# Routing counts over four token tiles per matmul, list products over two, and a new order at the start of the expert stage

## The chip, the cores and the metric

The kernel runs on one core of one Trainium2 chip. TensorE (PE) multiplies matrices, VectorE (DVE) and ScalarE (ACT) work element by element, GpSimd (POOL) does element work and issues the indirect DMAs, and SyncE (SP) issues the other DMAs. Each engine takes its own instructions in order and waits for the others by semaphores. The metric is the device time of one execution in microseconds; a span is the part of it that the profile shows.

## The reference

A linear attention (3072 tokens in all, 8 heads of 48) feeds an MLP (384 to 2048 to 384, leaky ReLU), and that feeds a mixture of 8 experts (384 to 1024 to 384, ReLU). The experts have a capacity of 384 tokens each, and the assignment is greedy over all pairs of token and expert:

```python
logits = x @ w_gate
order = np.argsort(-logits.flatten())
for idx in order:
    tok, e = int(idx) // E, int(idx) % E
    if assigned[tok] >= 0 or counts[e] >= cap:
        continue
    assigned[tok] = e
    counts[e] += 1
for e in range(E):
    mask = assigned == e
    out[mask] = np.maximum(x[mask] @ w1[e], 0.0) @ w2[e]
```

## The kernel before

The attention and the MLP come first; the MLP works on groups of 512 and at last 256 tokens. Every float32 product is split into high and low parts, so three matmuls stand for one.

**Routing.** Since every expert has room for just 384 tokens, the assignment is worked out as eight rounds, `route(p)` for p from 0 to 7. A round finds the expert that fills up first, its threshold, its members, and the list of their rows. Tokens lie on 128 partitions in 24 tiles. `close(p)` (line 811) narrows the threshold in 4 steps of 32 levels. A step compares each token's key with the levels (`G`, L826), counts for each expert how many tokens reach each level by 24 matmuls, one for each token tile, with the one-hot of the token's best expert as weights (`cnt`, L831), and turns the counts into the number of levels at which an expert is still full (`fl`, `Je`, `jt`, `Jm`, L836 to L840). The one-hot stands four times over, in four blocks of 32 columns, so that each block of 32 partitions gets the same counts. Then the keys are shifted (L842). After the last step the expert's number `ei`, the membership `memb` (L859) and its prefix sums `px` follow. `lists` and `compact` turn members into slots (`xi`), two one-hots `oa` and `A`, 24 matmuls (`ip`, L920), four small ones (`iw`, L926), and the row indices `idx` (L935). `next_picks` takes the members out and makes the next one-hot `oh`, which `spread` writes (L765, L766).

**Slots.** All this is written as a generator: each `yield` ends a slot, and whoever calls `next` puts a slot at that place in the engines' order. `first_route` runs route 0 against the rest of the MLP's second layer: after slot n it issues `REST[n]` steps of three matmuls (L636). Route 0 also starts the loads of the first expert's w1 on SP as soon as `ei` is known, and splits the first pieces.

**The start of the experts.** `experts` first issues the three gathers of rows (`xg`, L1111, one for each 128 tokens, on POOL), and then follows `START`, letter by letter: c is a slot of the next routes, w splits a weight piece into high and low (ScalarE copy L1104, POOL subtraction L1105), d issues the four w2 loads (L1097), t transposes a tile of x on TensorE (L1125) and copies it on ScalarE (L1127), and l forms its low part on VectorE (L1131).

**The expert loop.** For each expert p and each of its 8 blocks f of hidden units (j = 8p + f): a slot, layer 1 (L1141, 9 matmuls of 384 columns), another slot, layer 2 of two blocks earlier (L1158, 9 matmuls), then `hl` on VectorE (L1149). So route p + 1 runs in the slots beside expert p. When its indices are known, the next gathers are issued; x is transposed in the last two blocks before the expert starts. `put` (L1161) evacuates a finished expert's three output tiles and scatters them by indirect DMA (L1167).

## Time and profile before

| | us |
|---|---|
| median of 3 runs | 808.16 (806.79 to 810.96) |
| the profiled execution | 805.67 |
| its span | 803.9 |
| TensorE busy | 771.4 |
| VectorE busy | 569.8 |
| ScalarE busy | 405.6 |
| POOL busy | 282.0 |

The MLP's last group ends at about 538 us of the span, route 0 runs from about 521 to 544, and the experts' layers from 552 to the end. [...] In a timeline each row is a start, a duration, an engine, a line, the operation, what it writes and reads, and in brackets the idle time of the engine just before with what ended it.

### The profile page before, as it was taken

How to read it: one execution, taken by the hardware profiler on the slowest of the kernel's cores; microseconds unless marked ns; L12 is line 12 of the kernel's file. 1: busy time of each engine (PE TensorE's matmuls, PEld its weight loads, DVE VectorE, ACT ScalarE, POOL GpSimd, SP SyncE). 2: the span in 40 equal slices, each digit the busy share in tenths (PEclk: the TensorE clock that was granted, in tenths of full speed). 3: DMA queues.
4: the chain of work that ended last, by engine and by line, in shares of the span. 5: the costliest groups of instructions: out<-in, count | busy, mean ns of one | idle time of the engine just before them, and what ended most of it. 6: DMA issues, size and time to landing. Idle time of an engine off the chain costs nothing.

```text
span 803.9 us, 16531 instructions
## 1 busy us (share of the span) xinstructions
PE 771.4 (96%) x6139; PEld 709.6 (88%) x6139; DVE 569.8 (71%) x1536; ACT 405.6 (50%) x875; POOL 282.0 (35%) x275
## 2 busy tenths in 40 slices
PE   7999999999999999999999999986999999999996
PEld 6788887988999899988998999876899889899996
DVE  6999997897999989889884345656666666663221
ACT  4889895665444444444534455614344344344431
POOL 7888852322000000000000000016567675578661
PEclk9999999999999999999999999997999999999999
DMA  8798864512000200300200010034462462444400
GB/s 250 200 278 247 235 195 142 194 40 80 1 1 1 79 1 11 109 20 21 71 28 1 0 60 21 1 120 138 138 201 86 148 199 78 157 158 135 142 31 32
DMA packets 64584, 81.38 MB, mean 101 GB/s; under 512 B 8048, under 2 KB 55408, under 8 KB 64368
## 3 DMA queue, kind: packets, MB, share of 16 engines
q1 hardware_dynamic: 61008, 70.81, 28.3%
q0 software_dynamic: 3072, 9.44, 3.4%
q8 instruction: 50, 0.82, 0.4%
q14 instruction: 38, 0.31, 0.1%
q10 hardware_dynamic: 416, 0.00, 0.0%
HBM read 66.07 MB, written 14.16 MB: 100 GB/s over the span
## 4 chain that ended last, share of the span: by engine, by line
PE 72%; DVE 6%; issue 3%; POOL 1%; ACT 1%; another core or an unknown queue 0%; POOLq 0%; ACTq 0%; DVEq 0%
PE m L636 25%; PE ph L689 23%; PE eph L1141 10%; PE o L1158 9%; PE cnt L831 2%; PE ept L1125 1%; DVE gh L704 1%; DVE G L826 1%; POOL out_dram L1167 1%; POOL wbl L1105 1%; ACT nt L693 1%; DVE hl L1149 1%; PE ip L920 0%; ACT gh L694 0%; DVE oa L914 0%
## 5 line engine op out<-in xcount | busy, mean ns | idle before, releaser
L689 PE MATMUL ph<-xh,wah 128*128 128x512 f32 (+1 forms) x336 | 122.2, 364 | 0.8 <-ACTq L242 0.7
L689 PE MATMUL ph<-xl,wah 128*128 128x512 f32 (+1 forms) x336 | 121.9, 363 | 0.0
L689 PE MATMUL ph<-xh,wal 128*128 128x512 f32 (+1 forms) x336 | 121.8, 363 | 0.0
L693 ACT ACTIVATE nt<-ph 128x512 f32<-128x512 f32 (+1 forms) x112 | 60.1, 536 | 120.1 <-PE ph L689 109.6
L636 PE MATMUL m<-wbh,gl 128*128 128x384 f32 (+1 forms) x352 | 119.1, 338 | 0.5 <-DVE gl L715 0.5
L636 PE MATMUL m<-wbh,gh 128*128 128x384 f32 (+1 forms) x352 | 119.3, 339 | 0.0
L636 PE MATMUL m<-wbl,gh 128*128 128x384 f32 (+1 forms) x352 | 119.2, 339 | 0.0
L781 POOL COPY L<-M 128x176 f32<-128x176 f32 (+1 forms) x2 | 0.7, 357 | 329.4 <-DVE M L642 308.4
L704 DVE SCALAR_TENSOR_TENSOR gt<-nt,al,gt 128x512 f32<-128x512 f32 (+1 forms) x96 | 67.8, 706 | 50.6 <-ACT gt L694 50.6
L712 ACT CAST gh<-gt 128x512 fp32r<-128x512 f32 (+1 forms) x96 | 56.4, 587 | 72.1 <-DVE gt L704 71.2
L1144 ACT ACTIVATE hh<-eph 128x384 fp32r<-128x384 f32 x64 | 31.4, 491 | 118.5 <-PE eph L1141 108.7
L1149 DVE SCALAR_TENSOR_TENSOR hl<-eph,hh 128x384 fp32r<-128x384 f32 x64 | 35.6, 556 | 73.2 <-ACT hh L1144 72.1
L560 DVE SCALAR_TENSOR_TENSOR junk<-wt,wgb 128x384 f32<-128x384 f32 x128 | 71.3, 557 | 3.9
L689 PEld LDWEIGHTS ph<-xh,wal 128*128 128x128 f32 x336 | 63.1, 188 | 11.0
L1105 POOL TENSOR_TENSOR wal<-raw,wah 128x768 fp32r<-128x768 f32 x32 | 58.3, 1847 | 37.3 <-ACT wah L1104 35.1
L689 PEld LDWEIGHTS ph<-xh,wah 128*128 128x128 f32 x336 | 63.1, 188 | 9.1 <-ACTq L242 1.0
L715 DVE TENSOR_TENSOR gl<-gt,gh 128x512 fp32r<-128x512 f32 (+1 forms) x96 | 61.7, 643 | 12.7 <-ACT gh L712 12.6
L689 PEld LDWEIGHTS ph<-xl,wah 128*128 128x128 f32 x336 | 63.2, 188 | 7.6
L1105 POOL TENSOR_TENSOR wbl<-raw,wbh 128x768 fp32r<-128x768 f32 x32 | 58.5, 1847 | 32.0 <-ACT wbh L1104 22.4
L636 PEld LDWEIGHTS m<-wbh,gh 128*128 128x128 f32 x352 | 66.0, 188 | 3.5
L636 PEld LDWEIGHTS m<-wbl,gh 128*128 128x128 f32 x352 | 66.1, 188 | 3.3
L636 PEld LDWEIGHTS m<-wbh,gl 128*128 128x128 f32 x352 | 66.1, 188 | 0.9 <-DVE gl L715 0.9
(252 smaller groups left out, 1778.5 us busy)
## 6 DMA issues: line engine op xcount, KB each, us to landing
raw<-in_moe_w_dram SPq DMA_DIRECT2D x64, 384.0 KB
raw<-in_moe_w_in_dram SPq DMA_DIRECT2D x16, 384.0 KB
raw<-in_moe_w_out_dram SPq DMA_DIRECT2D x16, 384.0 KB
raw_r<-in_rt_dram SPq DMA_DIRECT2D x24, 224.0 KB
raw_k<-in_kc_dram SPq DMA_DIRECT2D x24, 192.0 KB
raw_v<-in_vc_dram SPq DMA_DIRECT2D x24, 192.0 KB
xd<-ysb SPq DMA_DIRECT2D x48, 96.0 KB
md<-raw SPq DMA_DIRECT2D x22, 192.0 KB
```

The costliest lines, as they stand in the source:

```text
L560: v.scalar_tensor_tensor(junk, t, 1.0, self.wgb[:, e], op0=ALU.mult, op1=ALU.mult, accum_out=wc[:, f, e:e + 1])
L636: nc.tensor.matmul(acc[t][:, :N], a[:, o], self.wb[b][:, f, :N], start=(f == 0 and n == 0), stop=(f == NF - 1 and n == 2))
L689: nc.tensor.matmul(ph[:, :T], self.wa[a][:, k, fs], b[:, k, :T], start=(n == 0), stop=(n == 8))
L693: nc.scalar.activation(nt[:, :T], ph[:, :T], AF.Relu, scale=-1.0)
L704: v.scalar_tensor_tensor(gt[:, :T], nt[:, :T], self.al[:, f:f + 1], gt[:, :T], op0=ALU.mult, op1=ALU.add)
L712: nc.scalar.copy(h, g)
L715: v.tensor_sub(l, g, h.bitcast(F32))
L1105: self.nc.gpsimd.tensor_sub(to[1], d, to[0].bitcast(F32))
L1141: self.nc.tensor.matmul(ph, w1[a][:, k, f * P:(f + 1) * P], x[b][:, k], start=(n == 0), stop=(n == 8))
L1144: self.nc.scalar.activation(hh, ph, AF.Relu)
L1149: self.nc.vector.scalar_tensor_tensor(hl, ph, 0.0, hh.bitcast(F32), op0=ALU.max, op1=ALU.subtract)
L1158: self.nc.tensor.matmul(self.acc[q], h[a][:, o], w2[b][:, f], start=(f == 0 and n == 0), stop=(f == NS - 1 and n == 2))
```

## The change

The count matmul takes four token tiles at a time: the weights hold 4 copies of a block of 4 tiles by 8 experts, the moving side 4 tiles by 32 levels, so 6 matmuls of 128 columns make a product, of whose 4 by 4 blocks the diagonal ones are wanted. VectorE transposes the 128 by 128 product in blocks of 32 by 32, which brings levels onto partitions, sums the diagonal over the four tiles (`tot`), takes the maximum over experts (`top`), transposes it, and counts the levels that are still full (`fl`, `Jm`). In the last step the flags are formed for each expert and turned back (`F`, `Je`, `jt`). All levels are compared, 32 instead of 31, with a level that no key reaches.

The list product takes two tiles at a time: 12 matmuls of 48 columns; two small copies take the diagonal, and `two`, two identities on top of each other, adds them in `iw`.

Of the slots, `lists` joins two into one; the part of `next_picks` that forms the next one-hot becomes `next_ones` and comes behind the indices, and from p = 2 on `next_picks` has a slot of its own. The expert loop takes a slot less at its first block, and asks for new indices in both slots of a block. At the start, `REST`, `PRE` and `START` are new, and the four w2 loads come first in `START`, each behind a small POOL memset of its buffer, which stands in POOL's queue behind the gathers. `put` copies all three tiles on ScalarE. The one-hots are no longer zeroed beforehand.

```diff
@@ -36,14 +36,14 @@
...
 NS = F2 // P
-REST = (1, 2, 1, 2, 1, 3, 1, 3, 2, 4, 4, 4) + (0,) * 4
+REST = (1, 2, 3, 2, 3, 2, 3, 3, 4, 0, 0, 5) + (0,) * 4
 TAIL = 1
-START = "cwwccccdtltltlc"
+START = "dcccwtwltclwtlc"
 HOLD = 2
...
 WARM = (8, 8, 4, 4)
-PRE = 2
+PRE = 1
 BASE = 6
@@ -131,19 +131,21 @@
...
         v.tensor_scalar(self.io1, io[:, :TH], 1.0, None, op0=ALU.add)
+        g.memset(self.io1[:, TH - 1:], BIG)
         self.pcol = cp.tile([P, 1], F32, name="pcol")
...
         for i in range(2):
-            t = self.rp.tile([P, NTT, 4, 32], BF, name=f"ohr{i}")
-            for a in range(0, NTT, 6):
-                g.memset(t[:, a:a + 6].rearrange("p a b e -> p (a b e)").bitcast(F32), 0.0)
-            self.ohr.append(t)
+            self.ohr.append(self.rp.tile([P, NTT // 4, 4, 4 * E], BF, name=f"ohr{i}"))
+        self.F = cp.tile([P, 32], F32, name="F")
+        g.memset(self.F, 0.0)
+        self.two = cp.tile([2 * TH, TH], F32, name="two")
+        v.tensor_tensor(self.two, self.ident[:2 * TH, :TH], self.ident[:2 * TH, TH:2 * TH], op=ALU.add)
         S = self.S = self.ps.tile([P, 512], F32, name="S")
...
         self.xi, self.bi5, self.ai5 = (S[:, 96 + 24 * i:120 + 24 * i].bitcast(I32) for i in range(3))
-        self.iot = S[:, 168:192]
+        self.iot, self.jt = S[:, 168:192], S[:, 192:224]
         v.memset(S[:, 56:58], 0.0)
@@ -759,31 +761,44 @@
...
         t = self.ohr[i % 2]
-        if act is None:
-            nc.vector.tensor_copy(t[:, :, 0, :E], eq)
-        else:
-            nc.vector.tensor_tensor(t[:, :, 0, :E], eq, self.bc3(act, E), op=ALU.mult)
-        nc.scalar.copy(t[:, :, 1:, :E], t[:, :, 0:1, :E].to_broadcast([P, NTT, 3, E]))
+        nc.vector.tensor_tensor(self.first(t), self.fours(eq),
+                                act.rearrange("p (k g) -> p k g", g=4).unsqueeze(3).to_broadcast([P, NTT // 4, 4, E]),
+                                op=ALU.mult)
+        nc.scalar.copy(t[:, :, 1:], t[:, :, 0:1].to_broadcast([P, NTT // 4, 3, 4 * E]))
         return t
 
+    def first(self, t):
+        return t[:, :, 0].rearrange("p k (g e) -> p k g e", g=4)
+
+    def fours(self, a):
+        return a.rearrange("p (k g) e -> p k g e", g=4)
+
     def picks(self, a, b):
...
         v = self.nc.vector
-        key, eq, oh, w = self.kap[:, a:b], self.eq[:, a:b], self.oh[:, a:b], b - a
+        key, eq, w = self.kap[:, a:b], self.eq[:, a:b], b - a
         M = self.M[:, a:b]
...
         yield
-        v.tensor_copy(oh[:, :, 0, :E], eq)
-        self.nc.scalar.copy(oh[:, :, 1:, :E], oh[:, :, 0:1, :E].to_broadcast([P, w, 3, E]))
+        for c, d in ((a, b - b % 4), (b - b % 4, b)) if a % 4 == 0 else ((a, b),):
+            if a % 4 == 0 and d % 4 == 0:
+                o, e4, sh = self.oh[:, c // 4:d // 4], self.eq[:, c:d].rearrange("p (k g) e -> p k (g e)", g=4), \
+                    [P, (d - c) // 4, 3, 4 * E]
+                v.tensor_copy(o[:, :, 0], e4)
+                self.nc.scalar.copy(o[:, :, 1:], o[:, :, 0:1].to_broadcast(sh))
+            elif d > c:
+                o = self.oh[:, c // 4, :, E * (c % 4):E * (c % 4) + E * (d - c)]
+                v.tensor_copy(o[:, 0], self.eq[:, c:d].rearrange("p t e -> p (t e)"))
+                self.nc.scalar.copy(o[:, 1:], o[:, 0:1].to_broadcast([P, 3, E * (d - c)]))
         self.nc.gpsimd.tensor_copy(self.L[:, a:b], M)
...
             n = min(6, b - i)
-            v.tensor_tensor(self.G0[:, i:i + n, :TH - 1], self.bc3(self.kap[:, i:i + n], TH - 1),
-                            self.bc1(self.T[:, 0, :TH - 1], n), op=ALU.is_ge)
+            v.tensor_tensor(self.G0[:, i:i + n], self.bc3(self.kap[:, i:i + n], TH), self.bc1(self.T[:, 0], n),
+                            op=ALU.is_ge)
             yield
@@ -815,32 +830,41 @@
...
         for s in range(STEPS):
-            n = TH if s == last else TH - 1
             if p == s == 0:
...
                 G = rp.tile([P, NTT, TH], BF, name="G")
-                cuts = (0, NTT // 2) if p == 0 else (0,)
-                for t in cuts:
-                    w = NTT // len(cuts)
-                    v.tensor_tensor(G[:, t:t + w, :n], self.bc3(kap[:, t:t + w], n), self.bc1(self.T[:, s, :n], w),
+                w = NTT // 2 if p == 0 else NTT
+                for t in range(0, NTT, w):
+                    v.tensor_tensor(G[:, t:t + w], self.bc3(kap[:, t:t + w], TH), self.bc1(self.T[:, s], w),
                                     op=ALU.is_ge)
             yield
-            cnt = self.pc.tile([P, TH], F32, tag="cnt", name="cnt")
-            for t in range(NTT):
-                nc.tensor.matmul(cnt[:, :n], oh[:, t].rearrange("p b e -> p (b e)"), G[:, t, :n],
-                                 start=(t == 0), stop=(t == NTT - 1))
+            cnt = self.pc.tile([P, 4, TH], F32, tag="cnt", name="cnt")
+            for k in range(NTT // 4):
+                nc.tensor.matmul(cnt, oh[:, k].rearrange("p r x -> p (r x)"), G[:, 4 * k:4 * k + 4],
+                                 start=(k == 0), stop=(k == NTT // 4 - 1))
             yield
-            fl = rp.tile([P, TH], BF, name="fl")
-            Je = rp.tile([P, 1], F32, name="Je")
-            v.tensor_scalar(fl[:, :n], cnt[:, :n], float(CAP), None, op0=ALU.is_ge, op1=ALU.add, accum_out=Je)
-            jt = rp.tile([P, 32], F32, name="jt")
-            v.transpose(jt, Je.to_broadcast([P, 32]))
+            tr = rp.tile([P, 4 * (TH + E)], F32, name="tr")
+            v.transpose(tr[:, :P], cnt.rearrange("p g n -> p (g n)"))
+            tot = rp.tile([P, E], F32, name="tot")
+            v.tensor_reduce(tot, tr.rearrange("p (g x) -> p x g", g=4)[:, :E], axis=AX, op=ALU.add)
             Jm = rp.tile([P, 1], F32, name="Jm", bufs=2)
-            v.tensor_reduce(Jm, jt[:, :E], axis=AX, op=ALU.max)
             if s < last:
+                top = rp.tile([P, 1], F32, name="Je")
+                v.tensor_reduce(top, tot, axis=AX, op=ALU.max)
+                v.transpose(self.jt, top.to_broadcast([P, 32]))
+                fl = rp.tile([P, TH], F32, name="fl")
+                v.scalar_tensor_tensor(fl, self.jt, float(CAP), self.ones48[:, :TH], op0=ALU.is_ge, op1=ALU.mult,
+                                       accum_out=Jm)
                 v.scalar_tensor_tensor(kap, Jm.to_broadcast([P, NTT]), self.nd[:, s:s + 1], kap, op0=ALU.mult,
                                        op1=ALU.add)
+        v.tensor_scalar(self.F[:, :E], tot, float(CAP), None, op0=ALU.is_ge)
+        v.transpose(self.jt, self.F)
+        Je = rp.tile([P, 1], F32, name="Je")
+        v.tensor_reduce(Je, self.jt, axis=AX, op=ALU.add)
+        jt = rp.tile([P, 32], F32, name="jt")
+        v.transpose(jt, Je.to_broadcast([P, 32]))
+        v.tensor_reduce(Jm, jt[:, :E], axis=AX, op=ALU.max)
         v.tensor_scalar(sel, jt[:, :E], Jm, None, op0=ALU.is_equal)
@@ -852,7 +876,8 @@
...
         po3 = rp.tile([P, NTT, E], F32, name="eq")
-        v.tensor_tensor(po3, oh[:, :, 0, :E], self.bc1(sel), op=ALU.mult)
+        v.tensor_tensor(self.fours(po3), self.first(oh),
+                        sel.unsqueeze(1).unsqueeze(1).to_broadcast([P, NTT // 4, 4, E]), op=ALU.mult)
         po = rp.tile([P, NTT], F32, name="ch")
@@ -863,11 +888,16 @@
...
 
-        v, rp = self.nc.vector, self.rp
+        v = self.nc.vector
         v.tensor_tensor(self.act, self.act, self.memb, op=ALU.subtract)
...
             v.tensor_reduce(self.kap, self.M, axis=AX, op=ALU.max)
+
+    def next_ones(self, p):
+
+        v, rp = self.nc.vector, self.rp
+        if p < E - 2:
             eq = rp.tile([P, NTT, E], F32, name="eq")
@@ -896,7 +926,6 @@
...
         v.scalar_tensor_tensor(self.xi, memb, 32.0 * BASE32, self.u, op0=ALU.mult, op1=ALU.add)
-        yield
         yield from self.compact(sc[:, NTT - 1:])
@@ -915,15 +944,17 @@
...
         yield
-        ip = self.pc.tile([TH, 2, NSL], F32, tag="cnt", name="ip")
-        for t in range(NTT):
-            nc.tensor.matmul(ip, oa[:, t], A[:, t], start=(t == 0), stop=(t == NTT - 1))
-        yield
-        is_ = rp.tile([TH, 2, NSL], F32, name="is_")
-        v.tensor_copy(is_, ip)
+        ip = self.pc.tile([2 * TH, 2, 2, NSL], F32, tag="cnt", name="ip")
+        for t in range(0, NTT, 2):
+            nc.tensor.matmul(ip, oa[:, t:t + 2].rearrange("p t a -> p (t a)"), A[:, t:t + 2], start=(t == 0),
+                             stop=(t == NTT - 2))
+        yield
+        is_ = rp.tile([2 * TH, 2, NSL], F32, name="is_")
+        for i in range(2):
+            v.tensor_copy(is_[TH * i:TH * i + TH], ip[TH * i:TH * i + TH, i])
         iw = self.pc.tile([P, 2, 3], F32, tag="cnt", name="iw")
         for g in range(4):
-            nc.tensor.matmul(iw[TH * g:TH * (g + 1)], self.ident[:TH, :TH],
+            nc.tensor.matmul(iw[TH * g:TH * (g + 1)], self.two,
                              is_.rearrange("a v (q g) -> a v q g", g=4)[:, :, :, g], start=True, stop=True)
@@ -986,7 +1017,7 @@
...
         v.tensor_reduce(mx, eq, axis=AX, op=ALU.max)
-        OH = self.ohr[0][:, :, 0, :E]
+        OH = rx.tile([P, NTT, E], BF, name="OH")
         v.tensor_tensor(OH, eq, self.bc3(mx, E), op=ALU.is_equal)
@@ -1077,7 +1108,7 @@
...
 
-    def wload(self, ei, s, late=None):
+    def wload(self, ei, s, behind=False):
 
@@ -1090,11 +1121,11 @@
...
             else:
-                if c == NP // 2 and late:
-                    e = late.value_load(ei[0:1, 0:1], min_val=0, max_val=E - 1)
+                if behind:
+                    nc.gpsimd.memset(raw[:1, :1], 0.0)
                 i = c - NP // 2
                 d = raw.rearrange("p (k f) -> p k f", k=2)
-                (late or nc.sync).dma_start(d, self.w2[bass.ds(e, 1), i * 256:(i + 1) * 256, :].rearrange(
+                nc.sync.dma_start(d, self.w2[bass.ds(e, 1), i * 256:(i + 1) * 256, :].rearrange(
                     "o (k p) f -> p (o k) f", p=P))
@@ -1162,7 +1193,7 @@
...
             ob = self.fp.tile([P, DM], F32, name="ob", bufs=3)
-            (nc.vector.tensor_copy if q == 1 else nc.scalar.copy)(ob, self.acc[q])
+            nc.scalar.copy(ob, self.acc[q])
             nc.gpsimd.memset(self.spacer, 0.0)
@@ -1193,11 +1224,15 @@
...
         ls = self.lists(self.memb)
-        yield from cut(ls, 3 if p else 99)
+        yield from cut(ls, 2 if p else 99)
         if p < E - 1:
             self.next_picks(p)
+        if p > 1:
+            yield
         yield from ls
         self.idxs[p] = self.idx
+        if p < E - 1:
+            self.next_ones(p)
 
@@ -1206,9 +1241,9 @@
...
             if load is None and self.eis:
-                load = self.load = self.wload(self.eis.pop(0), 0)
+                load = self.load = self.wload(self.eis.pop(0), 0, True)
                 self.pieces = [next(load) for _ in range(NP // 2)]
-            elif len(self.pieces) > NP // 2 - PRE:
+            elif len(self.pieces) > NP // 2 - PRE and n > 10:
                 self.wsplit(self.pieces.pop(0))
@@ -1246,13 +1281,17 @@
...
             at(k, lambda: self.wsplit(self.pieces.pop(0)))
-        for j in range(E * NS):
-            p, f = divmod(j, NS)
+        def step():
             next(ch, None)
...
                         at(k, fn)
+
+        for j in range(E * NS):
+            p, f = divmod(j, NS)
+            if j:
+                step()
             for q in list(self.eis):
@@ -1261,7 +1300,7 @@
...
             l1 = self.layer1(f, x[p][0], w[0])
-            next(ch, None)
+            step()
             for fn in plan.pop((j, 0), ()):
```

## Rows read from the trace of the kernel before

**Rows 1.** The page, busy time, share of the span and instructions of each engine.
```profile
PE 771.4 (96%) x6139; PEld 709.6 (88%) x6139; DVE 569.8 (71%) x1536; ACT 405.6 (50%) x875; POOL 282.0 (35%) x275
```
**Rows 2.** Busy time by stretch: stretch, length, engines' busy us, granted clock, DMA share, GB/s.
```profile
530.00:560.00 30.00, 20.42 (x216) 19.15 (x215) 18.71 (x70) 10.52 (x17) 14.05 (x10) 0.83 0.44 146
```
**Rows 3.** Timeline of TensorE from 538 to 567 us.
```profile
539.65 0.75 PE L920 MATMUL ip<-A,oa 128*32 128x24 bf16 x24 [1.00 <-ACT A L911]
...
544.60 0.80 PE L831 MATMUL cnt<-G,ohr 128*128 128x31 bf16 x24 [3.70 <-DVE G L826]
...
552.10 1.31 PE L1141 MATMUL eph<-fxh,wah 128*128 128x384 f32 x3
...
566.73 0.80 PE L1141 MATMUL eph<-fxh,wah 128*128 128x384 f32 x3
```
**Rows 4.** Timeline of VectorE from 531 to 545 us.
```profile
531.83 0.25 DVE L859 SCALAR_TENSOR_TENSOR memb<-S,ch 128x24 bf16<-128x24 f32 x1
...
534.38 0.20 DVE L896 TENSOR_TENSOR_SCAN sc<-ones,px 128x24 f32<-128x24 f32 x1 [2.11 <-PE px L893]
...
541.43 0.16 DVE L935 SCALAR_TENSOR_TENSOR idx<-iw,pv 128x6 uint32<-128x6 f32 x1
```
**Rows 5.** Timeline of the DMA issues of SP and POOL.
```profile
539.92 2.19 SPq L1097 DMA_DIRECT2D raw<-in_moe_w_dram  x4
...
542.49 1.15 POOL L1111 DMA_INDIRECT xg<-md,idx  x1 [3.06 <-DVE M L869]
```
**Rows 6.** Busy time by stretch, one us while the gathers run.
```profile
545.00:546.00 1.00, 0.40 (x16) 0.32 (x13) 0.00 (x0) 0.84 (x2) 0.79 (x1) 0.50 1.11 415
```
**Rows 7.** The chain that ended last: start, duration, what; merged matmuls.
```profile
486.79 1.08 PE ph L689 x9
...
570.17 0.61 PE cnt L831 x24
...
591.05 1.59 PE eph L1141 x9
...
594.21 0.69 PE ip L920 x24
...
640.80 0.33 PE ept L1125 x3
```
**Rows 8.** Timeline of VectorE, a count step of route 2.
```profile
570.81 0.19 DVE L836 TENSOR_SCALAR_CACHE_REDUCE fl<-cnt 128x31 bf16<-128x31 f32 x1 [1.05 <-PE cnt L831]
...
571.04 0.21 DVE L838 STREAM_TRANSPOSE jt<-Je 128x32 f32<-128x32 f32 x1
571.29 0.16 DVE L840 TENSOR_REDUCE Jm<-jt 128x1 f32<-128x8 f32 x1
571.49 0.25 DVE L842 SCALAR_TENSOR_TENSOR S<-Jm,nd,S 128x24 f32<-128x24 f32 x1
571.77 0.93 DVE L826 TENSOR_TENSOR G<-S,T 128x744 bf16<-128x744 f32 x1
```
**Rows 9.** The page, groups of instructions: count, busy time, mean ns.
```profile
L1149 DVE SCALAR_TENSOR_TENSOR hl<-eph,hh 128x384 fp32r<-128x384 f32 x64 | 35.6, 556 | 73.2 <-ACT hh L1144 72.1
```
**Rows 10.** Waits of TensorE from 553 to 760: us, times, longest.
```profile
PE iw L926 <- issue: 1.5, 2, 1.3
...
PE cnt L831 <- DVE G L826: 1.3, 3, 0.7
PE ept L1125 <- DVE fxl L1131: 0.9, 1, 0.9
PE iw L926 <- DVE is__9262 L923: 0.7, 1, 0.7
PE ip L920 <- ACT A L911: 0.7, 1, 0.7
...
```
**Rows 11.** The chain at 600 us, and POOL's timeline beside it.
```profile
600.32 2.04 PE cnt L831 x24
...
600.87 0.97 POOL L1111 DMA_INDIRECT xg<-md,idx  x1 [0.30 <-issue]
```

## The prediction

> **What bounds the kernel now.** I read the page first, then the busy time by stage, then the order of time on each engine around the change. The page gives TensorE 96% of the span [rows 1]: time comes only from TensorE work that goes, or from its idle time. Of its 32.5 idle us, nearly a third lie in one stage [rows 2]: between 530 and 560 us TensorE is busy for 20.4 of 30 us, at a mean granted clock of 0.83. The expert stage after it is almost full, so there only TensorE's own work counts.
>
> The hole at 530 to 560 is a serial chain. TensorE waits 1.00 us for ScalarE's A before the list product, 3.70 us for G before the second route's first count, and starts the first layer (L1141) only at 552.10 [rows 3]. VectorE shows why: the membership is ready at 531.8, but the scan after it starts at 534.38, 2.11 us of it idle for px, because px is queued behind six steps of the MLP's rest on TensorE; the row indices come at 541.4 [rows 4]. [...] The transposes of x stand behind the second count product in TensorE's order.
>
> **The start, step by step.** A rest step is 3 matmuls of 384 columns; nine such take 1.59 us [rows 7], so 0.53 us. Up to px, before: 19 rest steps and 4 counts of 0.61 us [rows 7] from the first count on. After: 22 steps and 4 counts of about 0.38 us (next part), 11.7 + 1.5 = 13.2 us against 10.1 + 2.4 = 12.5 us plus some waiting. The count loop thus becomes TensorE's bound: 5 steps and a count are 3.0 us, VectorE's longer chain is 2.9 us. So px comes where it came before, and so does the scan, about 534.4; memb, whose chain grows by some 2 us over the loop, is ready at about 534.0, just in time. From the scan on the list is faster. Its VectorE part is unchanged and ends near 537.4; TensorE has 5 rest steps (2.65 us) beside it, so the list product starts at 537.4 instead of 539.65: A is now issued ahead of the MLP's last copy on ScalarE, so that wait goes. It takes 0.4 us instead of 0.7, one more small copy follows, and the indices come at about 539.1 instead of 541.4. First sum: 2.4 us earlier.
>
> The gather follows its indices by 0.9 us as now; the last MLP store and the w1 loads, both on SP's queue, may hold it until 541. The w2 loads wait on POOL memsets that stand behind the three gathers, so they start near 544; behind them on SP stands nothing until the next expert's loads. Their first use is after the first relu, near 550; the three w2-free gathers should land by 546.5. Transposes 0 and 1 now stand ahead of the second count, so TensorE no longer waits for G (544.6 + chain) before x. The three transposes, each with a 0.5 us ScalarE copy behind it, end near 547; the first layer starts at about 547.6 instead of 552.1. The count, final and list slots of route 1 come two half steps later, so by its membership wait (px), which I leave at the same time and 0.9 us long, a layer pair more is done. Layers 4 and 5 then follow without the waits that stand between them now, and the fifth layer 1 starts at 562.2 against 566.73 [rows 3]. **Term 1: -4.5 us.** If the gather holds to 543, it is -2; if the clock doesn't fall, -6.
>
> **Counts.** Six matmuls of 128 columns take the place of 24 of 31. No row has 128 bf16 columns. Below: six at today's rate of 0.025 us, 0.15 us. Above: the f32 transposes of 128 columns, three in 0.33 us, so 0.66 us, which would gain nothing. Between: 9 matmuls of 384 columns in 1.59 and 9 of 256 in 1.08 us [rows 7] give 0.057 us per 128 columns, so 0.063 us each, 0.38 us a product; I take this, since these stream one pass as bf16 does. 0.61 - 0.38 = 0.23 us, for the 20 counts of routes 2 to 6, all between layers: **term 2: -4.6 us** (bounds -9.2 and +1). [...]
>
> **List products.** 12 matmuls of 48 columns instead of 24 of 24 in 0.69 us [rows 7]. Below 12 x 0.029 = 0.35, above 12 x 0.063 = 0.75; I take 0.42, nearer the first, since 48 columns are nearer 24. Six products: **term 3: -1.6 us**.
>
> **What VectorE pays.** A count step now is, from start to start: flags 0.23 (with the accumulator read), transpose 0.25, maximum 0.20, keys 0.28, then G 0.93 [rows 8]. After: a 128-wide transpose, a sum over 32, a maximum, a transpose, flags, keys. A VectorE element costs (0.93 - 0.16)/(744 - 8) = 1.05 ns [rows 8], so the wide transpose is 0.31 us, 0.35 from start to start, and the sum 0.22. Chain: 0.35 + 0.22 + 0.20 + 0.25 + 0.23 + 0.28 = 1.53 us against 0.96: +0.57 (bounds +0.4, if width is free, and +1.9, if the wide transpose and the strided sum each cost what G does). Between two counts TensorE has two layers, 3.2 us [rows 7]; chain and G are 2.46 us, so the steps are hidden. Where the count stands behind a layer, hl (0.56 us [rows 9]) goes first: 3.0 to 3.1, and with a low_rows as well about 0.3 us over, in some 4 places: +1.2. The last step grows by about 1 us (flags over experts, three more small operations); three layers (4.8 us) cover chain, flags, memb and hl except about 0.3 us in 6 routes: +1.8. The next expert's one-hot (1.0 us) moves behind the indices, ahead of G: about 0.5 us in 3 routes: +1.5. Against this the waits of the steady part [rows 10]: the 2.2 us before iw go, because that one-hot stood ahead of is_; the 0.7 before ip, because oa is issued a slot earlier; of the 1.3 before cnt and 0.9 before ept I count half. -4.0 + 4.5 = **term 4: +0.5 us** (-5 to +9).
>
> **Late flags.** One count shows 2.04 us in the chain instead of 0.61, until VectorE's flags start, while POOL issues the gathers [rows 11]. [...] The row is near the gathers, so I count half of these waits away, and the other half is a rival.
>
> **The rest.** Two more small copies in the MLP's last group, +0.2 us, since TensorE waits for VectorE there. The zeroing of the one-hots (POOL, idle then) costs nothing. The evacuation that goes from VectorE to ScalarE is nothing with the stage's engines at two thirds or less; the memset in front of w2 is nothing while the gather is ahead. Sum: -4.5 - 4.6 - 1.6 + 0.5 + 0.2 = -10.0 us. Against the profiled execution (805.67, span 803.9) 795.7; the median shown, 808.16, lies 2.5 us higher, so I say 798.
>
> **Rivals.** (a) The lateness stays: each of five gathers then delays a count by 1.5 us; 1.5 + 2.5 against 3.2 leaves 0.8 us, five times, less the half I counted: about +5, so 802 to 803. [...] (b) The start gains little, since the gather is bound by the MLP's store and by POOL's issue of 1.15 us each: -1 instead of -4.5, 801.5. For it the SP queue, which carries w1 and then the store; against it 415 GB/s of w2 that no longer run beside it. (c) Slower: VectorE's count chain becomes the bound of the expert stage. Its place is the wait of each count for G; it decides when chain and G exceed 3.2 us, that is when the chain grows by over 1.3 us, or by over 0.75 where hl stands in front. The wide transpose out of PSUM and the strided sum at G's price would do it: +1.9, so 0.6 and 1.15 us over, 0.9 in the mean, 18 us in 20 counts. With the waits before px and G (+3.5) and terms 1 to 3 (-10.7) that is +11: 819. Against it: the present transpose takes 0.21 us and the present maximum 0.16 [rows 8]. (d) The change doesn't do what it says: 128 columns at the f32 transposes' price, terms 2 and 3 at their upper bounds (+1 and +0.4): 805 to 806. (e) The waits all go and no new one comes: term 4 is -5, 793.
>
> **How the numbers follow.** A measurement of this kernel can tell about 0.5%, 4 us, from no change. The forecast, 794 to 801, has 0.52; (a) 0.12, (b) 0.06, (e) and better 0.10: faster together 0.80. (d), and (a) with (b) together, give 804 to 812: 0.12. (c) 0.08. The range from 790 to 805 leaves out (c), half of (e)'s lower end and part of the middle, about 0.2.
>
> **What would show it.** Right: the first L1141 near 547.5, the first gather ahead of the w2 loads; six count matmuls in 0.35 to 0.4 us; VectorE from product to keys in about 1.5 us; TensorE's waits for G under 0.5 us each. Wrong: waits for G or px of over 1 us in every route (then (c)); flags or the wide transpose that start late whenever POOL issues gathers (a); the transposes of x waiting for data past 548 (b).

## The result

The changed kernel takes 803.51 us, median of 8 runs (799.43 to 804.75); the kernel before, run beside it, 809.36 (806.79 to 814.02, 8 runs). The ratio is 0.9913, 95% interval 0.9885 to 0.9941: faster by 5.85 us. That lies inside the range of 790 to 805, above the 794 to 801 that had the most chance, and is little over half of the 10 us of the sum.

The profiled execution of after (span 802.3, time 804.11) reaches the first routing count at 524.69 us, that of before at 520.92. The granted clock (TensorE's, as the trace shows it, 1.00 being full speed) over the first 100 us makes this difference: it was 0.93 in this execution and 1.00 in that one, and e5 below, whose code up to the first count is that of after, reaches the count at 519.24 with the clock at 1.00. Executions of one kernel differ in it too (mean clock 0.978 to 0.987 in the eight of after). So times are counted from the first count's first product: to the end 277.61 us in after, 282.98 in before, -5.4, which agrees with the medians.

Page of after, busy time by engine; then the hole at the start [rows 1, 2]:
```profile
PE 769.6 (96%) x5539; PEld 706.0 (88%) x5539; DVE 589.3 (73%) x1601; ACT 409.6 (51%) x884; POOL 279.5 (35%) x273
```
```profile
530.00:560.00 30.00, 21.33 (x137) 18.70 (x135) 21.55 (x77) 8.65 (x15) 12.02 (x12) 0.77 0.43 139
```
The hole is no smaller: TensorE is still busy for only 21 of 30 us (20.6 in the 30 us that correspond to before's by the first count), at a lower mean clock, 0.77 against 0.83.

After, TensorE's timeline [rows 3] and VectorE's [rows 4]:
```profile
541.45 0.56 PE L949 MATMUL ip<-A,oa 128*64 128x48 bf16 x12 [0.31 <-DVE oa L943]
546.51 0.80 PE L844 MATMUL cnt<-G,ohr 128*128 128x128 bf16 x6 [3.71 <-DVE G L839]
550.15 1.59 PE L1156 MATMUL o<-ident,xg 128*128 128x128 f32 x6 [2.84 <-DMA xg<-md,idx]
553.85 1.33 PE L1172 MATMUL eph<-fxh,wah 128*128 128x384 f32 x3 [0.83 <-ACT fxh L1158]
...
569.00 0.79 PE L1172 MATMUL eph<-fxh,wah 128*128 128x384 f32 x3
```
```profile
538.45 0.20 DVE L926 TENSOR_TENSOR_SCAN sc<-ones,px 128x24 f32<-128x24 f32 x1
...
543.31 0.17 DVE L966 SCALAR_TENSOR_TENSOR idx<-iw,pv 128x6 uint32<-128x6 f32 x1
```
Take 3.77 us off each start to set it beside before. The list product waits 0.31 instead of 1.00 us, the indices come at 539.54 instead of 541.43. But TensorE now waits 2.84 us for the gathered rows; the first layer comes 2.0 us earlier, the fifth 1.5.

After, DMA issues of SP and POOL [rows 5], then busy time by stretch of 1 us (the two columns before the last: granted clock, DMA share):
```profile
537.71 2.27 SPq L1121 DMA_DIRECT2D raw<-in_moe_w_dram  x4
542.21 0.34 SPq L650 DMA_DIRECT2D md<-gt  x1
...
546.22 1.15 POOL L1142 DMA_INDIRECT xg<-md,idx  x1 [2.52 <-DVE ohr L764]
```
```profile
543.00:544.00 1.00, 0.00 (x0) 0.00 (x0) 0.83 (x6) 0.00 (x0) 0.70 (x1) 1.00 1.05 379
544.00:545.00 1.00, 0.00 (x0) 0.00 (x0) 0.90 (x4) 0.00 (x0) 0.00 (x0) 0.71 0.15 55
545.00:546.00 1.00, 0.00 (x0) 0.00 (x0) 0.97 (x3) 0.47 (x1) 0.00 (x0) 0.50 0.00 0
```
The gather starts at 546.22, 2.7 us behind its indices, where it stood in before (542.45 with the shift taken off, against 542.49). Ahead of it the w1 loads and the MLP's store (542.21) fill the DMA engines until about 544.2, and the store's last byte moves at 544.65. The bracket names VectorE's one-hot; experiments below ask whether that is the cause.

After, the chain that ended last [rows 7] and TensorE's waits in the expert stage, 557 to 764 us [rows 10: us, times, longest]:
```profile
655.43 0.49 PE ip L949 x12
661.24 0.35 PE cnt L844 x6
...
690.21 0.50 PE cnt L844 x6
```
```profile
PE cnt L844 <- DVE G L839: 2.9, 5, 1.1
PE px L922 <- DVE memb L884: 2.1, 3, 1.4
PE ept L1156 <- DVE fxl L1162: 1.9, 1, 1.9
```
A count is 0.35 us, or 0.50 where its start stands alone (mean of 16 rows 0.42, against 0.59 to 0.75, mean 0.64 of 18 undisturbed rows); a list product 0.49 against 0.69. The old waits, before iw and ip, are gone; px and ept have longer ones, and the second of these is dearer than it looks:
```profile
706.00:708.00 2.00, 0.63 (x5) 0.64 (x6) 1.83 (x9) 0.05 (x2) 0.00 (x0) 1.00 0.01 4
708.00:710.00 2.00, 2.00 (x9) 1.88 (x7) 1.55 (x5) 1.90 (x3) 0.76 (x1) 0.57 0.66 180
710.00:712.00 2.00, 2.00 (x10) 1.81 (x9) 1.33 (x6) 0.00 (x0) 2.00 (x2) 0.58 0.86 261
```
Behind it the granted clock falls from 1.00 to a mean of 0.57 over 4 us (0.50 from 708.5 to 711.5): by estimate 4 x 0.43 = 1.7 us more. VectorE's and POOL's timelines at the two longest waits show what made them late:
```profile
645.84 1.61 DVE L861 TENSOR_SCALAR F<-tot 128x8 f32<-128x8 f32 x1
...
674.48 0.17 DVE L861 TENSOR_SCALAR F<-tot 128x8 f32<-128x8 f32 x1
...
703.61 1.58 DVE L861 TENSOR_SCALAR F<-tot 128x8 f32<-128x8 f32 x1
```
```profile
645.55 5.44 POOL L1136 TENSOR_TENSOR wbl<-raw,wbh 128x768 fp32r<-128x768 f32 x3 [2.77 <-ACT wbh L1135]
...
703.32 1.84 POOL L1136 TENSOR_TENSOR wbl<-raw,wbh 128x768 fp32r<-128x768 f32 x1 [0.78 <-ACT wbh L1135]
```
F, the new flags over eight experts, takes 0.17 us in two other routes (and 0.25 and 0.66 in the last two of the six). At the two longest waits it ends at 647.45 and 705.19, where POOL's running subtraction ends (645.55 + 5.44/3 = 647.36, and 705.16). The profile shows this wait as busy time of F, not as idle time before it. The transposes and reductions around it run on beside POOL: from 647.48 to 648.38, under its subtractions, two transposes take 0.23 and 0.21 us and two reductions 0.19 and 0.16, as in the route at 674, where POOL stands idle beside them.

### The profile page after: what moved, and what is told of

Its sections match the earlier page's. It is cut to its first block, busy times and chain, and to the rows that moved or that the text cites. A ratio compares the mean times of both kernels' runs of the same rounds, so it can differ in the third digit from the quotient of the medians.

```text
span 802.3 us, 15416 instructions
## 1 busy us (share of the span) xinstructions
PE 769.6 (96%) x5539; PEld 706.0 (88%) x5539; DVE 589.3 (73%) x1601; ACT 409.6 (51%) x884; POOL 279.5 (35%) x273
## 4 chain that ended last, share of the span: by engine, by line
PE 69%; DVE 7%; issue 3%; ACT 2%; POOL 1%; DMA 1%; POOLq 0%; SPq 0%; another core or an unknown queue 0%; ACTq 0%; DVEq 0%
PE m L638 25%; PE ph L691 24%; PE eph L1172 9%; PE o L1189 9%; PE cnt L844 1%; DVE G L839 1%; PE ept L1156 1%; DVE gh L706 1%; POOL wbl L1136 1%; POOL out_dram L1198 1%; DVE fxl L1162 1%; ACT nt L695 1%; PE ip L949 1%; DMA xg<-md,idx 0%; DVE F L861 0%
```

## The experiments

All of them. The ratio comes from the runs, each set beside before on its own chip; the rest from one profiled execution of each kernel, in us from the first count (gather: start of the first one; layer 1: its first product; L5: relu of the fifth layer, which writes hh):

```
kernel               ratio to before [95%]     gather  layer 1   L5    L5 to end  to end
before               1                          21.57   31.18   47.8    235.2    282.98
after                0.9913 [0.9885, 0.9941]    21.53   29.16   46.2    231.4    277.61
e1_order             0.9965 [0.9946, 0.9984]    21.79   29.13   45.3    234.6    279.92
e2_products          1.0011 [0.9985, 1.0038]    22.90   32.30   53.0    233.4    286.38
e3_ones              0.9929 [0.9899, 0.9959]    22.47   29.85   47.0    229.9    276.92
e4_store             0.9930 [0.9903, 0.9956]    21.86   29.19   46.3    231.6    277.86
e5_F                 0.9946 [0.9923, 0.9968]    21.89   29.26   46.4    229.7    276.06
e6_F_products        1.0018 [0.9998, 1.0038]    23.02   32.29   52.8    233.2    285.98
e7_w1                0.9929 [0.9908, 0.9950]    20.22   28.18   45.3    231.3    276.56
e8_nohold            0.9947 [0.9923, 0.9970]    21.99   31.57   48.7    230.0    278.63
e9_Fpsum             0.9842 [0.9805, 0.9879]    22.86   30.17   47.2    225.6    272.82
e10_Fpsum_products   0.9916 [0.9880, 0.9952]    22.79   32.28   50.7    227.0    277.65
e11_Fpsum_w1         0.9850 [0.9813, 0.9887]    20.40   28.36   45.4    227.0    272.41
e12_warm             0.9886 [0.9850, 0.9922]    20.39   27.54   43.9    224.3    268.12
```

**The two halves of the change.** e1 is after with the old spread, picks, close and list product; e2 is after's products with before's constants, slots and loads.
```diff
-START = "dcccwtwltclwtlc"
+START = "cwwccccdtltltlc"
...
-                load = self.load = self.wload(self.eis.pop(0), 0, True)
+                load = self.load = self.wload(self.eis.pop(0), 0)
```


> The changed order alone: the kernel after with the counts and list products as they were before (24 matmuls each, VectorE's old chain, no extra small copies). Theory S (the order earns only the start, the products earn the steady part): fifth layer 1 about 1.5 us earlier against the first count than before, the stretch from there to the end as long as before (237 us, within 1 us), a median some 1.5 us under before's. Rival W (the order removes the waits before iw, px and ept, and the products only pay for their longer VectorE chain): the stretch to the end is 3 to 4 us shorter, the median 5 us under before's.

> The two products alone: the kernel before with six count matmuls of 128 columns, the new VectorE chain and 12 list matmuls, and with its old order, old slots and w2 loads not held. Theory S: the stretch from the fifth layer 1 to the end is some 4 us shorter than before (20 counts by 0.26 and 6 lists by 0.2 are 6.4 us of TensorE; 2.4 us of it lost in longer waits), the start as before, the median 4 us under before's. Rival W: the longer chain stands in the old slots, so waits for G and px grow by 3 us and more; the median lies within 1.5 us of before's or above it.

Neither theory holds for both halves. The order alone earns 0.35%, nearly all at the start, as S said, though more than S had there (2.5 of its 3.1 us lie ahead of L5). The products alone earn nothing, as W said: from L5 to the end e2 is 1.8 us shorter than before, but up to L5 it is 5.2 us longer. TensorE saves its work, and in e2 waits for it elsewhere, first at px:
```profile
561.13 0.20 PE L917 MATMUL px<-memb,tri 128*128 128x24 bf16 x1 [3.41 <-DVE memb L884]
```
In e2, F takes 1.5 to 1.6 us in three of six routes and 0.6 in two. So the halves don't add: 0.35% and nothing are 0.87% together.

**What holds the gather.** Three candidates: VectorE's one-hot, the store's queue, the bytes ahead of the store.
```diff
-        if p < E - 1:
+        if 0 < p < E - 1:
             self.next_picks(p)
...
         turns = add(0, self.idxs[0])
+        self.next_picks(0)
+        self.next_ones(0)
```


> The kernel after; the first route's masking of M, its maximum and the next expert's one-hot are issued behind the first gather, not ahead of it (order on VectorE itself unchanged). Theory O (the first gather waits until VectorE has done all that is issued ahead of it, and so for the one-hot, 545.49): the gather starts 0.9 us after its indices, about 2.0 us earlier against the first count than in the kernel after, the wait of the transposes for x falls from 2.8 to about 1 us, the time falls by 1.5 to 2 us. Rival M (it waits for the MLP's last store, which lies behind the w1 loads on SP's queue): the gather starts where it did, within 0.3 us, and the time is that of the kernel after.

```diff
-                    nc.sync.dma_start(self.md[tt * P:(tt + 1) * P], ms)
+                    last = gi == late and t == T - 1
+                    (nc.scalar if last else nc.sync).dma_start(self.md[tt * P:(tt + 1) * P], ms)
```


> The kernel after; the MLP's last store is issued from ScalarE's queue, so it does not lie behind the w1 loads on SP's queue. Rival M (the store holds the gather): the gather starts 1 to 2 us earlier against the first count, and the time falls by about as much. Theory O (the one-hot on VectorE holds it): the gather starts where it did, within 0.3 us, and the time is that of the kernel after.

Neither edit does what its theory said: the gather came 0.9 and 0.3 us later than in after, not earlier. In e4 the store is alone on ScalarE's queue:
```profile
539.95 0.36 ACTq L651 DMA_DIRECT2D md<-gt  x1
```
It still moved its bytes only from 541.5 to 543.0, with w1's until 542.5: the w1 loads had the engines.

```diff
-                self.pieces = [next(load) for _ in range(NP // 2)]
+                self.pieces = [next(load) for _ in range(2)]
...
+        self.pieces.extend(next(load) for _ in range(NP // 2 - 2))
```


> The kernel after; two of the four w1 loads of the first expert are issued behind the MLP's last store, not ahead of it. Theory B (the store shares the DMA engines with the w1 loads, whatever queue issues it, lands 2.8 us after its issue, and the gather waits for that and then for its queue): the store lands 1 to 1.5 us earlier, the gather starts 17 us after the first count's start and 20.3 us or less (21.5 in the kernel after), the first layer about 1 us earlier, the time falls by 0.5 to 1 us. Rival C (the gather waits for something on another engine): the gather starts 21.3 to 21.7 us after the first count, the time as in the kernel after.

DMA issues of e7, on SP and POOL:
```profile
541.07 0.34 SPq L650 DMA_DIRECT2D md<-gt  x1
541.67 1.00 SPq L1121 DMA_DIRECT2D raw<-in_moe_w_dram  x2
...
544.06 1.15 POOL L1142 DMA_INDIRECT xg<-md,idx  x1 [1.50 <-DVE eq L902]
```
The store's last byte moves 18.8 us after the first count, against 20.0 in after. The gather comes 1.3 us earlier (20.22 against 21.53), the first layer 1.0, the whole 1.05: theory B. (20.40 and 20.39 in e11 and e12, which have the edit too, against 21.5 to 22.9 in the others with the new order.) The time alone, 0.9929 against 0.9913, cannot show 1 us.

The DMA packets of the other traces say the same. In all fourteen kernels the gather starts 1.4 to 1.8 us after the store's last byte, while that byte itself lies anywhere from 18.8 to 21.4 us after the first count: in e3 both are 0.9 us later than in after, in e9 both 1.3. So the store holds the gather in every one, in before too (19.8 and 21.57), and the brackets, which name seven different rows in the fourteen, don't tell. In e7 the store's last byte and the indices come together (18.8 both), so that an earlier store alone would not bring the gather forward.

```diff
-                load = self.load = self.wload(self.eis.pop(0), 0, True)
+                load = self.load = self.wload(self.eis.pop(0), 0)
```


> The kernel after without the four POOL memsets that hold the first w2 loads behind the gathers. Theory B (the gather is held by the store; what matters further is that nothing fills the DMA engines while its rows move): the w2 loads start right behind the store, the gather starts as late as in the kernel after or up to 0.5 us later, its rows land 1 to 2 us later, the first layer starts 1 to 2 us later. Rival D (the hold is worth nothing, since the w2 bytes run beside the gather anyway): first layer and time within 0.3 us of the kernel after.

SP's DMA issues in e8:
```profile
538.84 0.34 SPq L650 DMA_DIRECT2D md<-gt  x1
539.43 3.28 SPq L1128 DMA_DIRECT2D raw<-in_moe_w_dram  x4
```
The w2 loads stand right behind the store. The gather starts 0.5 us later than in after, but the first layer 2.4: its rows move beside w2, until 28.3 us after the first count instead of 27.0. At the start the hold is worth that, somewhat more than B said; the stretch to the end shows 1.0, since this execution is spared the fall of the clock that after had.

**What holds F.**
```diff
-        v.tensor_scalar(self.F[:, :E], tot, float(CAP), None, op0=ALU.is_ge)
+        v.scalar_tensor_tensor(self.F[:, :E], tot, float(CAP), self.ones48[:, :E], op0=ALU.is_ge, op1=ALU.mult)
```


> The kernel after with one instruction in another form: the flags F over experts (L861, 128x8, SBUF to SBUF) by scalar_tensor_tensor with a row of ones in place of tensor_scalar. Theory P (a plain tensor_scalar waits for POOL's subtraction of a weight piece; F took 0.66, 1.6 and 1.6 us instead of 0.17 in routes whose F met one): all six F take about 0.2 us, the waits of px for memb (1.4 us at 650) and of the transposes for fxl (1.9 us at 707) shrink by 1.3 us or vanish, and the fall of the clock behind the second goes with it (some 1.7 us): from the fifth layer to the end 3 to 4.5 us less than the 231.4 of the kernel after. Rival Q (F is only where VectorE's read-after-write or a late count shows, whatever the form): F or the instruction behind it stays long in the same routes, the stretch stays at 230 to 232 us.

> The two products alone in the old order, with F in the new form. Theory P (the products alone earned nothing because F stood 1.5 us and more in three of six routes, with a wait of 3.4 us for px at the start): the wait for px falls from 3.4 to about 2 us, the waits for px, fxl and G in the steady part fall by 3 us, the ratio to before goes from 1.001 to about 0.995. Rival S (the old slots are too early for the longer chain, F apart): less than 1.5 us of change, ratio 0.999 and above.

VectorE's and POOL's timelines in e5:
```profile
698.30 1.58 DVE L861 SCALAR_TENSOR_TENSOR F<-tot,ones 128x8 f32<-128x8 f32 x1
```
```profile
698.01 1.84 POOL L1136 TENSOR_TENSOR wbl<-raw,wbh 128x768 fp32r<-128x768 f32 x1 [0.79 <-ACT wbh L1135]
```
F ends with POOL's instruction again (699.88, 699.85), so of rival Q "whatever the form" was right, not its reason, and e6, with the same hold, is e2 again. The 1.7 us between e5 and after are the clock: the same 1.9 us wait is there, without the fall behind it (nor in e3 and e8, where the clock stays at 1.00 as in e5; in e4 and e7 it fell to 0.50 over 2 us). Both forms have all their operands in SBUF.

```diff
-        self.F = cp.tile([P, 32], F32, name="F")
-        g.memset(self.F, 0.0)
...
-        self.iot, self.jt = S[:, 168:192], S[:, 192:224]
+        self.iot, self.jt, self.F = S[:, 168:192], S[:, 192:224], S[:, 224:256]
+        v.memset(self.F, 0.0)
```


> The kernel after with F in PSUM (a part of S, zeroed by VectorE) in place of SBUF; the instruction is the same tensor_scalar, 128x8. Theory P2 (F ends in every route with the end of POOL's running subtraction, as tensor_scalar with both sides in SBUF and as scalar_tensor_tensor with two inputs in SBUF; with PSUM on one side it needs nothing of POOL): all F take 0.15 to 0.3 us, the waits for memb (1.4) and fxl (1.9) fall to 0.5 us or less, from the fifth layer to the end 2.5 to 3.5 us less than the 229.7 us of the kernel with the other form. Rival Q2 (F is held wherever its sides lie): F stays at 1.6 us in two routes, the stretch at 229.7 to 231.4 us.

> The two products alone in the old order, with F in PSUM. Theory P2 (F's holds, 1.4 us in three of six routes and 0.5 in two, are why the products alone earned nothing): the wait for px in the first expert falls from 3.4 to about 2 us, those for fxl and memb from 3.9 to under 1 us; from the fifth layer to the end 3 us less than 233.4, ratio to before about 0.996. Rival S (the slots): from the fifth layer to the end 232 us or more, ratio 0.999 and above.

VectorE and POOL in e9, the route that was worst, then TensorE's waits from 557 to 764:
```profile
702.93 0.17 DVE L860 TENSOR_SCALAR S<-tot 128x8 f32<-128x8 f32 x1
```
```profile
702.65 1.84 POOL L1135 TENSOR_TENSOR wbl<-raw,wbh 128x768 fp32r<-128x768 f32 x1 [0.84 <-ACT wbh L1134]
```
```profile
PE cnt L843 <- DVE G L838: 3.1, 5, 1.2
PE px L921 <- DVE memb L883: 0.7, 2, 0.5
PE ept L1155 <- DVE fxl L1161: 0.5, 1, 0.5
```
With PSUM as its destination F takes 0.17 us in the middle of POOL's subtraction, and in all six routes. px waits 1.4 us less, ept 1.4, and the clock does not fall. e9's interval (0.9805 to 0.9879) lies clear of after's, e10's of e2's: theory P2. In e10, with the old order and the old slots, the products alone now earn 0.84%. TensorE's waits for px in e2, then in e10:
```profile
PE px L917 <- DVE memb L884: 4.9, 3, 3.4
```
```profile
PE px L916 <- DVE memb L883: 1.8, 2, 1.6
```
But the gain is larger than these waits. The relus of layers 49 and 61, with no route beside the layers between, in after and in e9:
```profile
741.42 0.49 ACT L1175 ACTIVATE hh<-eph 128x384 fp32r<-128x384 f32 x1 [1.17 <-PE eph L1172]
...
780.46 0.49 ACT L1175 ACTIVATE hh<-eph 128x384 fp32r<-128x384 f32 x1 [2.68 <-PE eph L1172]
```
```profile
737.52 0.49 ACT L1174 ACTIVATE hh<-eph 128x384 fp32r<-128x384 f32 x1 [1.15 <-PE eph L1171]
...
776.11 0.49 ACT L1174 ACTIVATE hh<-eph 128x384 fp32r<-128x384 f32 x1 [2.64 <-PE eph L1171]
```
These twelve layers take 39.0 to 39.1 us in every kernel from before to e8, and 38.6 in e9 to e12: 0.04 us a layer, by estimate 2.4 over the 60 from L5 on. So of the 4.1 us between e5 and e9 from L5 to the end (neither has the fall) about 2 are F's hold (TensorE's waits from L5 on are 5.0 us in e5 and 2.9 in e9) and about as much a faster pace.

What makes the pace is open. Taking F's tile away moved what lies behind it in SBUF, which no run tests by itself. e9 to e12 also ran on other chips than e1 to e8, but the traces speak against the chip: e12, on another one than e9 to e11, has their pace, and the MLP, from its first product ph to its last, is slower in all four than in after and e2 to e8 (393.6 against 392.9 us).

> The kernel after with F in PSUM and two of the four first w1 loads behind the MLP's last store. Both theories (F's hold in two routes; the store beside the w1 loads): from the first count to the end 277.6 - 1.1 - 3.5 = about 273 us, the ratio to before about 0.987. If the gains aren't added (a wait takes the place of F's), 275 to 276 us.

796.15 us, 0.985. The 272.4 us to the end meet the sum that was expected, but e9 has 272.8 without the w1 edit. Up to the last scatter the gains do add: it is issued 264.5 us after the first count, against 266.2 in e9. From there to the end this execution takes 7.9 us, and all thirteen others 6.6 to 6.8. With e9 (796.41) it is the version that beats both kernels; the two can't be told apart.

```diff
-START = "dcccwtwltclwtlc"
+START = "dc99ccw8twltclwtlc"
```


> The kernel with F in PSUM and the two late w1 loads, and in the hole at the start 26 extra TensorE products that nothing reads (18 behind the products of the first row indices, 8 ahead of the first transposes; 0.13 us each as at the kernel's start). Theory K (the hole's second price is the clock: it fell to 0.50 from 545 to 555 us, so nine products of a layer took 3.0 instead of 1.6 us, two counts 0.85 instead of 0.5): the granted clock stays at 1.00 through the hole, the gather starts where it did, the first layers take 1.6 us, from the first count to the end 2 to 2.5 us less than 272.4. Rival L (the extra work delays the count and the transposes, or the clock falls all the same): no change, or up to 1 us more.

Busy time by stretch in e11, then in e12 (the column of the clock is the third from the end):
```profile
552.00:554.00 2.00, 2.00 (x6) 2.00 (x7) 1.79 (x9) 0.00 (x0) 1.30 (x1) 0.50 0.85 304
```
```profile
546.00:548.00 2.00, 2.00 (x23) 1.99 (x22) 0.87 (x5) 0.65 (x1) 1.39 (x3) 1.00 0.50 149
...
552.00:554.00 2.00, 1.85 (x9) 1.53 (x9) 1.82 (x8) 0.09 (x1) 2.00 (x2) 1.00 0.96 303
```
The clock stays at 1.00, a layer's first three products take 0.79 instead of 1.33 us, and the fifth layer comes 1.5 us earlier: theory K for the clock. Two later waits for G (1.18 and 0.99 us, against one of 1.42 in e11) take part of it. What it is worth in all stays unclear. In the trace e12 takes 4.3 us less to the end than e11, but 2.7 of these lie behind L5, where K has no cause for them (1.3 are e11's slow end). In the runs its ratio, 0.9886, lies above e11's 0.985 with intervals that overlap, beside a before that takes 801.34 us on that chip and 808.63 on e11's.

## Why the prediction was nearly right

The direction and the range held; the sum was -10.0 us, and the trace has -5.4 from the first count on.

**Term 1, the start, failed: -1.5 instead of -4.5.** The chain up to the indices came as worked out (-1.9 against -2.4; scan and count steps where they were put). The step that failed is "The gather follows its indices by 0.9 us as now; the last MLP store and the w1 loads, both on SP's queue, may hold it until 541". SP's DMA issues in before:
```profile
531.79 2.27 SPq L1090 DMA_DIRECT2D raw<-in_moe_w_dram  x4
...
539.19 0.34 SPq L648 DMA_DIRECT2D md<-gt  x1
```
Here the w1 loads were through (538.5) before the store was issued, and the store's last byte (540.7) came 0.7 us ahead of the indices (541.4), so that the 0.9 us looked like a distance from the indices. The change brought the indices forward and put the w1 loads 2.1 us later against the first count, so that they were still moving when the store was issued. (Not only the longer count chain on VectorE does this: each half of the change alone does, 12.9 us after the first count in e1 and 13.0 in e2, against 10.9 in before.) So the second-latest input decided. The store was through at 540.9 on before's clock, near the 541 of the text; but the gather starts 1.4 to 1.8 us behind the store's last byte in every kernel, which the text did not count, so it started at 542.45 instead of about 541. The case "If the gather holds to 543, it is -2" is nearly what came: the first layer was 2.0 us earlier, the fifth 1.5. And the hold was put down to the queue where it was the DMA engines (e4 against e7). The gain that did come needs the hold of w2 (e8).

**Terms 2 and 3, the products, held:** 20 x (0.64 - 0.42) = -4.4 us against -4.6, and 6 x 0.20 = -1.2 against -1.6. The old and the new count were both taken 0.03 to 0.04 us too short, which cancels in the difference: there the sum was lucky. The text took 128 bf16 columns at the rate of the layers' matmuls (1.59 us for 27 x 128 columns, 0.059 each): a count of 0.35 us has it, 0.058, one of 0.50 us, whose start stands alone, 0.083.

**Term 4, the waits: +1.2 instead of +0.5, and made of other things.** All waits of TensorE over the stage [rows 10 and its smaller rows] were 7.4 us, and are 6.9, with 1.7 of clock on top. Those before iw and ip went, as forecast; those before cnt and ept, half counted as removed, grew. VectorE's chain is what was worked out: from a count's transpose to G 1.56 us (698.57 to 700.13), against 1.53. But the longest waits that came back, 1.4 us for px and 1.9 for ept with 1.7 of clock behind it, are not chain length; they are F held by POOL. "Late flags" asked what POOL holds of the old flags, which read PSUM, and not of the one new instruction that has both sides in SBUF; "What VectorE pays" counted F among the last step's small operations. With term 1 and the products that is -5.9; the trace has -5.4.

**Signs.** Of those it named, the first layer (550.1 on before's clock, not near 547.5) and the waits for G (up to 1.1 us, not under 0.5) went against it; the w2 loads behind the gathers, VectorE's chain and, where the start is hidden, the count (0.35 us) went with it.

**Rivals.** (a) fell: the new chain starts beside gathers (a transpose at 661.63, a gather from 660.80 to 661.76, the count's end at 661.59). (b) came true for the start, with the engines in the queue's place. (c) fell in after, since chain and G fit between two counts; but its engine is where the gain was lost, in F. In the old slots, too, it was F that took what the products earned: nothing in e2, 0.84% in e10 (the faster pace is part of that). (d) fell: a count takes 0.35 to 0.51 us, not 0.66. (e) did not come; with F in PSUM the total (796.4) came near it, in part by the pace that nobody had forecast.

## What to carry to other kernels

When one input of a wait is brought forward, list the others of that wait with their own times: the gain ends where the second-latest stands, and what shares its DMA engines counts, not only its queue (e4: issued at 539.95 on a queue of its own, the store moved its bytes from 541.5 on, beside w1's). Check each new elementwise VectorE instruction, however small, for where its operands lie while POOL runs: here 128x8 cost 1.6 us with both sides in SBUF and 0.17 with one side in PSUM. Price an idle TensorE twice, once for the wait and once for the clock that may fall behind it (here 1.9 us and, by estimate, 1.7; in e3, e5 and e8 it did not fall), and count from a point that the change can't reach when the stretch ahead of it varies by more than the change (here the first count came at 519.24 us in e5 and at 524.69 in after).

## What was not expected of the hardware

An elementwise VectorE instruction of 128x8 took 1.58 us and ended within 0.03 us of a running POOL instruction of 1.84 us, in two forms (after and e5), and took 0.17 us beside it with PSUM as its destination (e9); reductions and transposes between SBUF tiles ran beside the same POOL instructions at their usual 0.21 us.

A wait of 1.9 us on TensorE was followed by some 4 us at a mean clock of about 0.57 in after, and by a fall of the same kind in e4 (0.70, then 0.50 in stretches of 2 us) and e7 (0.50, then 0.72); in e3, e5 and e8, with the same instructions around it, the clock stayed at 1.00.

The pace of the layers with no route beside them, 3.17 us (after, 744.40 to 747.57) or 3.13 (e9, 740.46 to 743.59), differed between kernels that have the same TensorE instructions in them; it is not explained.

An indirect DMA that reads what a store wrote started 1.4 to 1.8 us after the store's last byte, in fourteen executions; a store of 192 KB, alone on its queue, was issued at 539.95 in e4 and moved its bytes from 541.5 to 543.0, while loads of another queue were moving until 542.5.
